# Long convolution and gated projection on one core: a GpSimd wait at the shared port, one pool of SBUF rooms, DRAM copies in another stage, GpSimd's tap in the last sequence

## The chip, the cores and the metric

The kernel runs on one core of a Trainium2 chip. The core has TensorE (in the profile PE for matrix products and PEld for weight loads), VectorE (DVE), ScalarE (ACT), GpSimd (POOL) and SyncE (SP, which here only issues DMAs). The metric is the device time of one execution in microseconds. All data are float32.

## The reference

For 8 sequences x of 6400 positions and 128 channels, the kernel computes a causal convolution with a filter h as long as the sequence (by Fourier transform), then a block with a short 5-tap convolution as gate and two 128 x 128 projections:

```python
L = 2 * S                                   # S = 6400
Xf = np.fft.rfft(x, n=L, axis=1)            # x: (8, 6400, 128)
Hf = np.fft.rfft(h, n=L, axis=0)            # h: (6400, 128)
x = np.fft.irfft(Xf * Hf[None], n=L, axis=1)[:, :S, :]
...
for k in range(5):
    gate_pre += conv_w[k][None, None, :] * xp[:, k:k + S, :]
gate = 1.0 / (1.0 + np.exp(-gate_pre))
val = x @ w_val
out = gate * val @ w_out
```

## The kernel before, in words

6400 is written as N1 x N2 = 100 x 64, and the transforms are products with constant matrices in four stages per sequence.

- **First stage** (`first_stage`, line 500): 16 groups of 8 channels. A group of x is loaded from DRAM into a room `x_sb` (4 rooms; at the start of the kernel 8 more in the place of the constant m4), TensorE makes 4 products of 200 columns, and ScalarE or VectorE copies the result into `gy`, in four pieces of 64x400.
- **Second stage** (`second`, line 546, and `product`, line 586): 13 blocks `kb` of 8 frequencies (the last has 4). A block needs a constant block `m2` (512 KB, `m2_load`, line 539) and the two blocks of the filter's spectrum (real and imaginary, 512 KB each, `h_load`, line 616), loaded from DRAM for every sequence. TensorE makes 8 products into two PSUM banks; ScalarE copies the result with halves swapped into a work room `w`; VectorE multiplies the PSUM result by the real part into `gy` (in the profile gy<-ps,h) and `w` by the imaginary part (w<-w,h); GpSimd adds the two (gy<-gy,w). In the last block VectorE adds.
- **Third stage** (loop over `q`, line 715): 32 groups of 4 products from `gy` into PSUM, copied to `dt` by ScalarE or VectorE. It starts when every add of the second stage is done. The first stage of the next sequence runs between its groups, since it writes `gy` where the third stage has read it.
- **Fourth stage** (loop over `CHUNKS`, line 827): 13 chunks of up to 5 cells of 100 positions. TensorE makes two products per cell with the constant `m4`; ScalarE copies the result to a room `y`; then come the taps: ScalarE starts sums in `dt` or `gl` (tap 4, and 3 as a product in `q`), VectorE adds three taps with scalar_tensor_tensor, and GpSimd adds `q` (dt<-dt,q or gl<-gl,q). In the last sequence VectorE adds four taps and GpSimd none. `gated` (line 786) follows for each chunk: sigmoid on ScalarE, projection by TensorE, gate on VectorE, second projection by TensorE, a copy out of PSUM and the store. The fourth stage and the next sequence's second stage run beside each other. Chunks with index `LAGGED` and above read `y` from SBUF and not the PSUM bank, and their taps and gate have due times in the next third stage.

**The head.** Before the first sequence the spectrum of h is computed by the same first two stages (`spectrum`, line 638) and stored to a DRAM tensor `hd`, and the first sequence's second stage runs beside it (`direct`, line 563). For blocks 0 to 4 both halves (64 partitions each) of the two planes are stored; for blocks 5 to 12 one half is, and a DRAM to DRAM copy doubles it (`hd<-hd`, lines 685 to 691, due times from `HEAD_END` on). Six groups of the next sequence's x (`STASH`) also go through the first stage here, into a part of m4's room.

**Rooms.** In SBUF there are 4 rooms for `m2` (`M2B`), 4 for h (`HB`) and 3 for `w` (`WB`), each 128 partitions x 4 KB. Each kind is used in turn: the n-th user waits for the (n - 4)th, or (n - 3)rd.

**What sets the order.** The program is a list of steps (`_Op`) with a cost, the steps that it follows, and a due time (`plan.base`). `_Plan.forward` (line 202) plays them through with modelled costs: each engine, when it is free, takes the ready step with the earliest due time that fits. The instructions are then issued to each engine in that order, and `_InOrder` (line 98) keeps it. On the chip each engine runs its own list in order; between engines there are only the waits that the data need. `port=True` marks steps whose VectorE or GpSimd instruction reads two operands in SBUF. The planner lets one of them run at a time and doesn't begin one on VectorE if the port is busy for over `PATIENCE` ns more (line 220). This is in the model alone: nothing on the chip ties GpSimd's instructions to VectorE's there.

```python
if o.port and e == "vector" and port > now + self.PATIENCE:
    return False
```

All instructions are issued through one helper, so every row of the profile has its line, L106; the rows are told apart by tile names and shapes.

Of the kernel before, what the change touches and what calls it, by code (L numbers as in the profile page):

```python
# [16 lines left out]
C = 128  # L17
# [17 lines left out]
LAGGED = 9  # L35
# [3 lines left out]
WB = 3  # L39
HB = 4  # L40
# [57 lines left out]
class _InOrder:  # L98
    def __init__(self, tc, engine):
        self._tc, self._engine = tc, engine  # L100

    def __getattr__(self, name):
        call = getattr(self._engine, name)

        def run(*args, **kwargs):
            return self._tc.keep_in_program_order(call(*args, **kwargs))  # L106

        return run


class _Engines:
    def __init__(self, tc):
        nc = tc.nc
        self.tensor, self.vector, self.scalar = (_InOrder(tc, e) for e in (nc.tensor, nc.vector, nc.scalar))
        self.gpsimd, self.sync = (_InOrder(tc, e) for e in (nc.gpsimd, nc.sync))
# [11 lines left out]

class _Op:
# [3 lines left out]
    def __init__(self, run, cost, after, bank=None, new=False, port=False):  # L132
        self.run, self.cost, self.bank, self.new, self.port = run, cost, bank, new, port
        self.after = [a for a in after if a is not None]
# [3 lines left out]
class _Plan:  # L138
# [4 lines left out]
    LEAD, LAND, AHEAD = 1500, 2000, 1200  # L143
# [58 lines left out]
    def forward(self):  # L202
# [3 lines left out]
        halves = [[0] * 2 for _ in range(4)]  # L206
        self.split = False
        port = server = now = 0
        events, began = [], []
        for o in self.ops:  # L210
            o.at = None
            if o.bank is not None:
                o.bank.left, o.bank.seen, o.bank.spot = len(o.bank.users), [], None

# [20 lines left out]
        while left:  # L235
            moved = True
            while moved:
                moved = False
                for e in free:
# [26 lines left out]
                    if o.port and e in ("vector", "gpsimd"):  # L266
                        port = now + dur
                    b = o.bank
                    if b is not None:
                        if o.new:  # L270
                            i, h = b.spot = self.room(b, halves, now)
                            self.split = self.split or b.n == 1
# [42 lines left out]
    def room(self, b, halves, now):  # L315
# [5 lines left out]
        if not self.split and not all(all(p) for p in free[2:]):  # L321
            return None
        spot = next(((i, h) for i in (2, 3) for h in (0, 1) if free[i][h]), None)
# [24 lines left out]
def _dma(kb):  # L348
    return 330, kb * 1024 / 400
# [7 lines left out]
def longconv_moe(ctx: ExitStack, tc: tile.TileContext, x, h, r1, m2, r3, m4, w64, out):  # L357
# [19 lines left out]
    y_t = [cp.tile([128, CH, N1], F32, name=f"y_{i}") for i in range(YB)]  # L377
    y_head = cp.tile([128, HEAD[1], N1], F32, name="y_head")
    m2_sb = [cp.tile([128, KB, C], F32, name=f"m2_{i}") for i in range(M2B)]
# [615 lines left out]
```

## Time and profile before

| what | us |
|---|---|
| median of 3 timed runs | 1075.39 (1075.15 to 1077.14) |
| the profiled execution, its own time | 1071.16 |
| span of its instructions | 1069.4 |
| outside the span | 1.76 |
| TensorE busy | 1046.7 |
| VectorE busy | 764.7 |
| ScalarE busy | 773.4 |
| GpSimd busy | 390.6 |

A row of a view by stretches has the stretch, its length, the busy time and the number of instructions (x) of each engine, the granted share of TensorE's clock (PEclk), the share of time that the 16 DMA engines are busy, and GB/s. A row of a group of instructions has engine, operation, what it writes and reads, shapes and count; then its busy time and the mean of one in ns; then the idle time of its engine ahead of it and what ended that. A row of the timeline has its start, its length, and in brackets the idle time before it and what ended it. A float32 product appears as two MATMUL and two LDWEIGHTS records.

The span falls into a head up to about 106 us; seven rounds of about 126 us (third stage of a sequence with the first stage of the next, then its fourth stage with the next one's second stage), of which the third stages begin at about 106, 216, 342, 467, 594, 720 and 846 us; and the last sequence, whose third stage begins at 971 us and which has no next one.

### The profile page before, as it was taken

Reading aid. Unit: us, or ns where it says so; the run is one execution under the profiler, and the core shown is the slowest. Engines: PE = TensorE matmul, PEld = TensorE weight load, DVE = VectorE, ACT = ScalarE, POOL = GpSimd, SP = SyncE. Lnnn points to the kernel's source line nnn. Section 1 sums busy time; section 2 is a strip of 40 time slices with the busy share of each in tenths; the row PEclk is TensorE's granted clock in tenths of the full one; section 3 lists DMA queues with packets and bytes.
Section 4 is the critical chain, followed back from the end, with each engine's and each line's share of the span. In section 5 each row is a group of like instructions: output and inputs, shape, how many; then the busy total and the mean of one; then the engine's idle time right before and its main releaser. Section 6 shows DMA issues by size and latency. Waiting matters only on the chain.

```text
span 1069.4 us, 19629 instructions
## 1 busy us (share of the span) xinstructions
PE 1046.7 (98%) x7488; PEld 941.8 (88%) x7488; DVE 764.7 (72%) x1059; ACT 773.4 (72%) x1282; POOL 390.6 (37%) x225
## 2 busy tenths in 40 slices
PE   9998999999999999999999999999999999999997
PEld 9998998889988899888988799888998889988983
DVE  6999259963698647985498835987379763997197
ACT  5687678866887669866787568876688666887553
POOL 0077107820286105750077201861048410674000
PEclk9999999999999999999999999999999999999999
DMA  9499939933498227962299424993269731891012
GB/s 270 135 361 364 280 85 355 365 135 87 148 383 318 92 83 258 381 215 97 78 348 373 132 88 124 375 335 107 80 217 385 246 95 47 298 331 49 27 49 76
DMA packets 80459, 221.14 MB, mean 207 GB/s; under 512 B 9514, under 2 KB 24846, under 8 KB 80142
## 3 DMA queue, kind: packets, MB, share of 16 engines
q1 hardware_dynamic: 80366, 219.89, 59.3%
q8 instruction: 59, 0.97, 0.4%
q14 instruction: 34, 0.28, 0.1%
HBM read 184.47 MB, written 39.32 MB: 209 GB/s over the span
## 4 chain that ended last, share of the span: by engine, by line
PE 74%; DVE 10%; DMA 8%; issue 3%; ACT 2%; POOL 1%; SPq 0%; DVEq 0%; POOLq 0%
PE pb L106 46%; PE ps L106 28%; DMA h<-hd 6%; DVE dt L106 3%; DVE gy L106 3%; DVE gl L106 2%; DVE w L106 1%; POOL gy L106 1%; ACT w L106 1%; DMA hd<-hd 1%; DMA m_sb<-hl 1%; DMA gl<-w 1%; ACT dt L106 1%; POOL gl L106 0%; DMA x<-xl 0%
## 5 line engine op out<-in xcount | busy, mean ns | idle before, releaser
L106 ACT COPY gy<-ps 64x400 f32<-64x400 f32 x436 | 211.9, 486 | 111.1 <-PE ps L106 107.3
L106 PEld LDWEIGHTS pb<-r_sb,gy 128*100 128x100 f32 x2048 | 239.4, 171 | 31.6 <-issue 24.4
L106 POOL TENSOR_TENSOR gy<-gy,w 128x1024 f32<-128x1024 f32 x96 | 230.9, 2406 | 76.9 <-DVE w L106 61.9
L106 PEld LDWEIGHTS pb<-m_sb,dt 100*128 100x128 f32 x1968 | 232.4, 193 | 19.6 <-issue 17.8
L106 PE MATMUL pb<-r_sb,gy 128*100 128x128 f32 x2048 | 245.7, 273 | 2.6 <-ACT gl L106 2.2
L106 PE MATMUL pb<-m_sb,dt 100*128 100x100 f32 x1968 | 234.3, 275 | 0.7 <-ACT dt L106 0.7
L106 DVE COPY dt<-pb 100x512 f32<-100x512 f32 x162 | 112.0, 691 | 149.5 <-PE pb L106 133.6
L106 PEld LDWEIGHTS ps<-gy,m 128*128 128x128 f32 x1600 | 194.9, 188 | 23.0 <-issue 16.3
L106 PE MATMUL ps<-gy,m 128*128 128x128 f32 x1600 | 201.5, 278 | 1.7 <-DVE gy L106 1.0
L106 PE MATMUL ps<-r_sb,x 100*128 100x200 f32 x992 | 186.9, 333 | 3.4 <-DMA x<-xl 2.2
L106 PEld LDWEIGHTS ps<-r_sb,x 100*128 100x128 f32 x992 | 165.8, 190 | 13.1 <-issue 11.0
L106 DVE SCALAR_TENSOR_TENSOR dt<-pb,w_sb,dt 128x500 f32<-128x500 f32 (+7 forms) x216 | 131.6, 626 | 9.0 <-issue 4.9
L106 DVE TENSOR_TENSOR w<-w,h 128x1024 f32<-128x1024 f32 (+1 forms) x91 | 119.3, 1311 | 12.5 <-DMA h<-hd 12.3
L106 DVE TENSOR_TENSOR gy<-ps,h 128x1024 f32<-128x1024 f32 (+1 forms) x100 | 117.3, 1176 | 10.2 <-DMA h<-hd 9.6
L106 ACT COPY y<-pb 128x500 f32<-128x500 f32 x136 | 77.1, 571 | 60.1 <-PE pb L106 51.9
L106 POOL TENSOR_TENSOR dt<-dt,q 128x500 f32<-128x500 f32 (+3 forms) x56 | 90.2, 1611 | 60.3 <-ACT w L106 41.9
L106 ACT ACTIVATE w<-ps 64x1024 f32<-64x1024 f32 (+1 forms) x91 | 89.9, 988 | 30.2 <-issue 18.7
L106 POOL MEMSET dt<- 128x4 f32 x8 | 0.8, 104 | 303.4 <-PE pb L106 303.4
L106 POOL TENSOR_TENSOR gl<-gl,q 128x500 f32<-128x500 f32 (+1 forms) x42 | 52.7, 1254 | 113.4 <-DVE gl L106 101.2
L106 PE MATMUL pb<-y,w_sb 128*128 128x500 f32 x178 | 91.1, 594 | 0.7 <-ACT y L106 0.7
L106 ACT COPY w<-ps 64x1024 f32<-64x1024 f32 (+1 forms) x91 | 88.4, 971 | 1.5
L106 DVE SCALAR_TENSOR_TENSOR gl<-y,w_sb,gl 128x500 f32<-128x500 f32 (+1 forms) x108 | 77.3, 727 | 13.3 <-POOL gl L106 10.8
(65 smaller groups left out, 915.2 us busy)
## 6 DMA issues: line engine op xcount, KB each, us to landing
h<-hd SPq DMA_DIRECT2D x168, 512.0 KB, 6.2
m<-m SPq DMA_DIRECT2D x96, 512.0 KB, 6.0
x<-xl SPq DMA_DIRECT2D x116, 224.0 KB, 2.6
out<-y SPq DMA_DIRECT2D x89, 250.0 KB, 4.5
hd<-h SPq DMA_DIRECT2D x8, 512.0 KB, 5.9
hd<-hd SPq DMA_DIRECT2D x14, 256.0 KB, 6.3
h<-hd SPq DMA_DIRECT2D x14, 256.0 KB, 4.5
m_sb<-xl SPq DMA_DIRECT2D x12, 224.0 KB, 6.6
```

The source lines that it names most:

```text
L106: return self._tc.keep_in_program_order(call(*args, **kwargs))
```

## The change

1. **GpSimd waits for VectorE at the port.** `_Engines` keeps a list of the instructions made. When the program is issued, a GpSimd step marked `port` gets a dependency, by semaphore, on the last instruction of the last VectorE step marked `port` that stands before it in the plan and has not been used for this yet.
2. **One pool of rooms.** The 4 + 4 + 3 rooms become 11 rooms `k_t` (`SLOTS`); a step that needs one takes any free room when the planner places it (`_Slot`, `take`), and it is free again when the last user is done. Loads leave one room free (`spare=1`); m2 still has at most 4 blocks at a time. The head has two rooms more, as before. The first rooms for x grow by four (in `y`), and the loads for the stash use them.
3. **The last adds.** `summed` may be placed on VectorE or GpSimd for block 11 of a second stage that has h loaded (`MANY = 2`); block 12 stays on VectorE.
4. **DRAM copies.** The copies that double blocks 5 to 12 are due in the first third stage, and each pair waits for a group of that stage, from the fifth on.
5. **The last sequence.** Chunks 1 to 9 (`LASTQ = 10`) have GpSimd's tap there too, ahead of VectorE's taps (`LAST3`). The last chunk is cut in two, of 3 and 2 cells. It has 11 + 6 rooms for y, as 7 + 6 before.
6. **The planner's numbers.** New due times, `LAGGED` 8 for 9, `LAST_LAG` 10 for 9, `PATIENCE` 380 for 143, one warming product less, `LAND` 2200 for 2000, a DMA at 375 for 400 bytes per ns. One-bank steps may take a free two-bank room before the small ones exist, and the first third stage may use the two-bank rooms.

```diff
-LAGGED = 9
+LAGGED = 8
...
-WB = 3
-HB = 4
+SLOTS = 11
+MANY = 2
...
-THIRD = 50165
-FOURTH = 5190
-SECOND = 4398
-GATE = 9690
-LAGS = 10092
-EARLY = -3528
-PATIENCE = 143
-ROUSE = 4
-LAST = 3839
-LAST_GATE = 8804
-LAST_LAG = 9
+THIRD = 44275
+FOURTH = 4511
+SECOND = 3959
+GATE = 13466
+LAGS = 9341
+EARLY = 545
+PATIENCE = 380
+ROUSE = 3
+LASTQ = 10
+FIRST3 = 0
+LAST3 = 1
+LAST = 3177
+LAST_GATE = 12434
+LAST_LAG = 10
...
+class _Slot:
+    def __init__(self, head=False):
+        self.users, self.head, self.place = [], head, None
...
+        def open_slots(o):
+            n = len(slots) if o.take.head else SLOTS
+            return [i for i in range(n) if slots[i] is not None and slots[i] <= now]
...
+            if any(s.spot is None for s in o.wait) or o.take is not None and len(open_slots(o)) <= o.spare:
+                return False
...
+                    if o.take is not None:
+                        i = o.take.spot = min(open_slots(o), key=lambda i: (i < SLOTS, slots[i]))
+                        slots[i] = None
+                    for s in [*o.use, *([o.take] if o.take else [])]:
+                        s.left -= 1
+                        if not s.left:
+                            slots[s.spot] = max(u.done for u in s.users)
...
-    m2_sb = [cp.tile([128, KB, C], F32, name=f"m2_{i}") for i in range(M2B)]
-    h_sb = [cp.tile([128, KB * C], F32, name=f"h_{i}") for i in range(HB)]
+    k_t = [cp.tile([128, KB * C], F32, name=f"k_{i}") for i in range(SLOTS)]
     x_sb = [cp.tile([PX, XG, N2], F32, name=f"x_{i}") for i in range(XB)]
-    w_t = [cp.tile([128, KB * C], F32, name=f"w_{i}") for i in range(WB)]
...
+    spare += [t[:PX] for t in y_sb[:4]]
...
+    def summed(kb, w, u, after, many):
+        where = {"gpsimd": _pool(count(kb) * C)}
+        if kb == NKB - 1:
+            where = {}
+        if kb >= NKB - many:
+            where["vector"] = _dve(count(kb) * C)
+        return add(
+            lambda e: getattr(nc, e).tensor_tensor(out=u, in0=u, in1=kdt(w.ap(), kb), op=ADD),
+            where, after, port=True, use=[w],
+        )
...
-    for g in range(NG):
-        kb = WHOLE + g
-        plan.where, plan.base = f"double {kb}", HEAD_END + 2500 * g
-        if kb < NKB:
-            n = count(kb) * C
-            lo, hi = slice(0, N2), slice(N2, 2 * N2)
-            stored[kb][0] = [dma(hd[kb, 0, hi, :n], hd[kb, 0, lo, :n], n // 4, stored[kb][0])]
-            stored[kb][1] = [dma(hd[kb, 1, lo, :n], hd[kb, 1, hi, :n], n // 4, stored[kb][1])]
+    def double(kb, after):
+        n = count(kb) * C
+        lo, hi = slice(0, N2), slice(N2, 2 * N2)
+        for r, (o, i) in enumerate(((hi, lo), (lo, hi))):
+            stored[kb][r] = [dma(hd[kb, r, o, :n], hd[kb, r, i, :n], n // 4, [*stored[kb][r], *after])]
...
+        for kb in range(WHOLE, NKB if b == 0 and nxt else 0):
+            plan.where, plan.base = f"double {kb}", begin + 2500 * (kb - WHOLE)
+            double(kb, [s3[4 + 2 * (kb - WHOLE)]])
...
+        chunks = CHUNKS if nxt else [*CHUNKS[:-1], (CHUNKS[-1][0], 3), (CHUNKS[-1][0] + 3, CH - 3)]
...
-            if nxt:
+            by_pool = nxt or i < LASTQ
+            if by_pool:
...
+            if not by_pool or not (FIRST3 if nxt else LAST3):
+                taps()
...
+                if FIRST3 if nxt else LAST3:
+                    taps()
...
+    held = None
     for op in plan_ops:
...
+        nc.made.clear()
         op.run(op.engine)
+        if op.port and op.engine == "vector":
+            held = nc.made[-1]
+        elif op.port and op.engine == "gpsimd" and held is not None:
+            tc.add_manual_dep(nc.made[0], held.name, sync, reason="the port is VectorE's")
+            held = None
```

More of the change, by code (lines that the diff above doesn't have):

```diff
@@ L125, in ap, with __init__ @@
         return self.place
+class _Slot:
+    def __init__(self, head=False):
+        self.users, self.head, self.place = [], head, None
+    def ap(self):
+        return self.place
 class _Op:
-    def __init__(self, run, cost, after, bank=None, new=False, port=False):
+    def __init__(self, run, cost, after, bank=None, new=False, port=False, take=None, use=(), wait=(), spare=0):
         self.run, self.cost, self.bank, self.new, self.port = run, cost, bank, new, port
+        self.take, self.use, self.wait, self.spare = take, list(use), [*use, *wait], spare
+        for s in [*self.use, *([take] if take else [])]:
+            s.users.append(self)
         self.after = [a for a in after if a is not None]
@@ L320, in room @@
             return next(((i, 0) for i, p in enumerate(free) if all(p) and (i < 2 or not self.split)), None)
-        if not self.split and not all(all(p) for p in free[2:]):
-            return None
-        spot = next(((i, h) for i in (2, 3) for h in (0, 1) if free[i][h]), None)
+        spot = None
+        if self.split or all(all(p) for p in free[2:]):
+            spot = next(((i, h) for i in (2, 3) for h in (0, 1) if free[i][h]), None)
         if spot is None and b.wide:
@@ L406, in spectral, with dma, run @@
         return bank.ap().rearrange("p b (k d t) -> p d (b k) t", t=2, d=C // 2)
-    def dma(o, i, kb, after=(), early=0):
-        return add(lambda e: nc.sync.dma_start(o, i), {"sync": _dma(kb)}, after, early=early)
+    def dma(o, i, kb, after=(), early=0, **more):
+        def run(e):
+            nc.sync.dma_start(*(a() if callable(a) else a for a in (o, i)))
+        return add(run, {"sync": _dma(kb)}, after, early=early, **more)
     def cells(y, n):
@@ new lines, in swap, with times_im @@
+            nc.scalar.activation(t[:N2], v[N2:], AF.Copy, scale=1.0 if kb < WHOLE else -1.0)
+            nc.scalar.copy(t[N2:], v[:N2])
+        def times_im(e):
+            t = kdt(w.ap(), kb)
+            nc.vector.tensor_tensor(out=t, in0=t, in1=kdt(hs[1].ap(), kb), op=MUL)
+        c = _times(_act(n, held=True), 2)
+        s = add(swap, {"scalar": (c[0] + 95, c[1])}, [p], bank=bank, take=w, wait=hs)
+        a = times_re(kb, p, bank, hs, u, h_ready[:1])
+        b = add(times_im, {"vector": _dve(n)}, [s, h_ready[1]], port=True, use=[hs[1], w])
@@ L625, in gy_at @@
+        return summed(kb, w, u, [a, b], MANY)
+    def h_load(kb):
+        k, hs = count(kb) * C, [_Slot(), _Slot()]
+        ops = []
+        for r, slot in enumerate(hs):
+            ops.append(dma(
+                lambda slot=slot: slot.ap()[:, :k], hd[kb, r, :, :k], k // 2, [*head_done, *stored[kb][r]], 6000,
+                take=slot, spare=1,
+            ))
+        return hs, ops
     def gy_at(g):
@@ L660, in spectrum @@
+        stored.append([[x] for x in st])
         return p, hs, [r0, r1_], [i0, i1], st
@@ L909, in part @@
                 return o, lambda: view(k, k + o.shape[1])
[L911 to L913 removed]
+            k4 = max(0, min(n, HEAD[0] - a - 4))
+            if k4:
+                first(4, [part(o, k) for k, o in cells(a + 4, k4)], gl_free(a + 4, k4), a + 4, k4)
+            by_pool = nxt or i < LASTQ
+            if by_pool:
                 qi = len(q_user)
```

212 lines of the change are left out of this document (96 added, 116 removed).

## The prediction

> **What bounds the kernel now.** I read the page first, then the busy time by stretches, then the timeline where TensorE (PE) is idle, then the groups of instructions.
>
> ```profile
> span 1069.4 us, 19629 instructions
> PE 1046.7 (98%) x7488; PEld 941.8 (88%) x7488; DVE 764.7 (72%) x1059; ACT 773.4 (72%) x1282; POOL 390.6 (37%) x225
> ```
>
> PE is busy 98% of the span, and the change neither adds nor removes a matrix product worth naming. So a gain can come only out of PE's idle time, 1069.4 - 1046.7 = 22.7 us, and out of stretches in which its clock is low. The next view cuts the span where the third stage of a sequence begins (six windows of 12 us, then 960), and at head and tail.
>
> ```profile
> core 0: us, PE busy (x) PEld busy (x) DVE busy (x) ACT busy (x) POOL busy (x), PEclk, DMA share, GB/s
> 0.00:94.00 94.00, 92.45 (x652) 90.86 (x653) 82.33 (x118) 67.71 (x100) 33.78 (x25) 1.00 0.82 270
> 94.00:106.00 12.00, 8.14 (x49) 7.15 (x48) 11.52 (x14) 8.66 (x17) 7.88 (x5) 1.00 1.00 378
> ...
> 206.00:218.00 12.00, 10.83 (x78) 9.00 (x78) 11.18 (x13) 7.43 (x12) 5.96 (x3) 1.00 0.98 342
> ...
> 332.00:344.00 12.00, 10.90 (x82) 9.20 (x81) 11.97 (x14) 8.10 (x14) 9.87 (x6) 1.00 0.93 333
> ...
> 457.00:469.00 12.00, 11.04 (x83) 9.34 (x83) 11.97 (x15) 8.09 (x14) 9.48 (x5) 1.00 0.93 324
> ...
> 582.00:594.00 12.00, 10.64 (x66) 8.68 (x64) 11.49 (x12) 5.64 (x10) 7.71 (x4) 0.86 0.86 286
> ...
> 710.00:722.00 12.00, 10.17 (x73) 8.34 (x72) 11.58 (x14) 6.95 (x13) 5.99 (x3) 1.00 0.81 264
> ...
> 834.00:846.00 12.00, 10.44 (x68) 8.85 (x67) 9.89 (x12) 5.75 (x10) 8.52 (x6) 0.86 0.84 300
> ...
> 960.00:972.00 12.00, 11.84 (x90) 10.15 (x89) 11.43 (x13) 8.70 (x15) 10.65 (x6) 1.00 0.26 86
> ...
> 1050.00:1066.00 16.00, 13.14 (x32) 5.02 (x31) 12.06 (x19) 6.18 (x13) 0.00 (x0) 0.89 0.21 77
> ```
>
> Window less PE's busy time: 1.55 us before 94; 3.86 us at 94 to 106; 1.17, 1.10, 0.96, 1.36, 1.83, 1.56 and 0.16 us at the seven boundaries, 8.14 in all; 2.86 us at 1050 to 1066. The clock is below 1 in three of these windows:
>
> ```profile
> 588.56:592.20 3.64, 3.64 (x13) 2.72 (x13) 3.60 (x5) 0.00 (x0) 2.41 (x2) 0.54 0.80 240
> 841.40:845.00 3.60, 3.60 (x12) 2.60 (x13) 3.35 (x5) 0.00 (x0) 2.37 (x2) 0.53 0.73 253
> 1059.70:1063.50 3.80, 3.80 (x6) 1.62 (x6) 1.49 (x3) 1.52 (x3) 0.00 (x0) 0.55 0.12 46
> ```
>
> 3.64 x 0.46, 3.60 x 0.47 and 3.80 x 0.45 are 1.7 us each, 5.1 in all: work that counts as busy and takes twice its time. So what can be won is 3.9 (head) + 8.1 + 3.4 (boundaries) + 2.9 + 1.7 (tail) = 20.0 us.
>
> **Why PE is idle at a boundary.** The third stage needs every product of the second stage, and the last of them are late:
>
> ```profile
> 581.57 1.51 DVE L106 TENSOR_TENSOR w<-w,h 128x1024 f32<-128x1024 f32 x1 [1.90 <-DMA h<-hd]
> 584.13 3.05 DVE L106 TENSOR_TENSOR w<-w,h 128x1024 f32<-128x1024 f32 x1
> 583.73 2.37 POOL L106 TENSOR_TENSOR gy<-gy,w 128x1024 f32<-128x1024 f32 x1
> 588.56 1.73 PE L106 MATMUL pb<-dt,w_sb 128*128 128x500 f32 x2 [1.36 <-ACT gl L106]
> L106 DVE TENSOR_TENSOR gy<-ps,h 128x1024 f32<-128x1024 f32 x92 | 111.9, 1219 | 10.2 <-DMA h<-hd 9.6 <-ACT q L106 0.3
> L106 DVE TENSOR_TENSOR w<-w,h 128x1024 f32<-128x1024 f32 x84 | 109.5, 1303 | 11.7 <-DMA h<-hd 11.5
> L106 POOL TENSOR_TENSOR gy<-gy,w 128x1024 f32<-128x1024 f32 x96 | 230.9, 2406 | 76.9 <-DVE w L106 61.9 <-PE ps L106 7.3 <-PE pb L106 7.1
> L106 POOL TENSOR_TENSOR dt<-dt,q 128x500 f32<-128x500 f32 x35 | 72.0, 2057 | 18.1 <-DVE dt L106 11.0 <-PE pb L106 2.8 <-ACT dt L106 2.2
> L106 DVE TENSOR_TENSOR w<-w,h x91: 804/1218/3049, 160.0 to 968.8; 128x1024 f32<-128x1024 f32 x84, 128x512 f32<-128x512 f32 x7
> L106 POOL TENSOR_TENSOR gl<-gl,q 128x500 f32<-128x500 f32 x35 | 45.0, 1285 | 113.4 <-DVE gl L106 101.2 <-ACT y L106 12.2
> ```
>
> VectorE (DVE) first waits 1.90 us for a block of h, then its next w product, 1.22 us long where nothing holds it (the same size from PSUM: 1219 ns), takes 3.05 us, because GpSimd's (POOL) add began 0.4 us earlier and holds the port to its end. 1.90 + 1.83 = 3.7 us of lateness leave PE idle for 1.36, and at 588.56, where that gap ends, the first low stretch begins. The other direction is dearer: GpSimd's tap takes 2057 ns where it meets such a product and 1285 where it mostly doesn't, 0.77 x 35 = 27 us of GpSimd's time in seven sequences.
>
> **The change, part by part.** *One pool of rooms.* The second stage is close to what DMA gives:
>
> ```profile
> 533.00:588.00 55.00, 53.80 (x404) 47.63 (x402) 49.57 (x59) 46.50 (x67) 40.66 (x21) 1.00 0.96 358
> 533.00:589.00 56.00, 41.66 (x21) 1.00 0.96 355
> h<-hd SPq DMA_DIRECT2D x168, 512.0 KB, 6.2
> ```
>
> (The second row is GpSimd alone.) Before, loads own 4 rooms for m2 and 4 for h, 8 in all, and 3 rooms lie empty between stages. After, loads may take all but one of 11: 10 rooms, 2 more, of 524 kB each. 1.05 MB at 355 GB/s are 3.0 us of DMA moved out of each second stage into the third, where DMA is not full. The 1.90 us wait above would be gone. *The last adds.* Block 11 may be added by DVE: about 1.3 us instead of 2.41, so the third stage can begin up to 1.1 us earlier. *The wait.* GpSimd waits for DVE's last port product before it in the plan. For an add that product is mostly its own input, so nothing changes; a tap waits by semaphore where it now waits at the port. It costs nothing where the port would have held it (cover: the 0.77 us), and the length of the product, up to 1.3 us, where GpSimd would have been first; what stands behind it are the next adds and taps on POOL, then sigmoid, gate and PE's projection. It takes reversals away, of which DVE shows (1303 - 1219) x 84 = 7.1 us. Chunk 8 is lagged now: three more products (0.73 us each) per sequence hold the port, and the plan lets DVE begin up to 0.38 us before the port is free (0.14 before). The other new constants set order alone.
>
> Boundaries together: between nothing and 8.1 + 3.4 = 11.5 us. Each gap (0.2 to 1.8 us) is shorter than the 3.0 us of DMA or 1.1 + 1.8 us of port that the change takes off its chain, but a new order brings gaps of its own (the bad end is the backfire, below). I take half of the idle time and both half-clock stretches: 4.1 + 3.4 = **-7.5 us**.
>
> *DRAM copies.* At the end of the head:
>
> ```profile
> 103.12 0.49 SPq L106 DMA_DIRECT2D hd<-hd  x1
> 103.77 0.46 SPq L106 DMA_DIRECT2D m<-m  x1
> 104.27 0.47 SPq L106 DMA_DIRECT2D hd<-hd  x1
> 105.71 1.08 PE L106 MATMUL ps<-r_sb,x 100*128 100x200 f32 x5 [2.23 <-DMA x<-xl]
> hd<-hd SPq DMA_DIRECT2D x14, 256.0 KB, 6.3
> 106.00:148.00 42.00, 42.00 (x335) 41.80 (x334) 13.36 (x20) 26.28 (x51) 5.11 (x6) 1.00 0.70 213
> ```
>
> The copies stand between the loads of x on SP's queue, at a DMA share of 1.00, and PE waits 2.23 us for x. After, they come from the fifth group of the third stage on, and x has four more rooms. I take the 2.2 us and leave the other 1.6 of the 3.86 (waits for evictions): **-2.2 us**, between 0 and -3.9. The third stage has room: 16 copies, each at most 0.26 MB read and 0.26 written, are 8 MB, 23 us at 355 GB/s at the very most and 11 if read and write overlap; 30% of 42 us is 12.6, and some copies lie in it already. On SP they are 16 issues of 0.49 us, 7.8 us of the stage, ahead of loads of x, m4 and h. If they don't fit, x or m4 is late there, for up to the 2.2 us that it cost before: the term is then 0.
>
> *Tail.* DVE is the late engine there, and the start is quoted beside it:
>
> ```profile
> 1059.69 1.03 PE L106 MATMUL pb<-gl,w_sb 128*128 128x500 f32 x1 [1.46 <-DVE gl L106]
> L106 DVE SCALAR_TENSOR_TENSOR gl<-y,w_sb,gl 128x500 f32<-128x500 f32 x100 | 73.5, 735 | 12.1 <-POOL gl L106 10.8
> L106 ACT ACTIVATE q<-pb,w_sb 128x500 f32<-128x500 f32 x56 | 38.2, 683 | 0.0
> 1.18 3.78 PE L106 MATMUL ps<-q 128*128 128x256 f32 x8 [1.18 <-DVE q L106]
> ```
>
> Nine chunks of the last sequence give one tap each (735 ns on DVE, 6.6 us in all) to GpSimd, which has nothing to do at 1050 to 1066; ScalarE gets nine activations of 683 ns, 6.1 us, spread over a stretch in whose last 16 us it is busy for 6.18. Taking 6.6 us off DVE ahead of the 1.46 us gap removes most of 2.9 + 1.7; the last chunks (one of them now in two pieces of 3 and 2 cells, some more small instructions) still go by DVE alone. **-3.0 us**, between +1.3 (GpSimd's tap, 1285 ns, now stands ahead of DVE's three, where no other chunk covers it) and -4.6. *The start*: one of four warming products less, of 3.78 us together, and x has then to be there 0.9 us sooner. I take 0, between -0.9 and +0.9 (the first real products at half the clock for as long).
>
> Sum: 7.5 + 2.2 + 3.0 = 12.7 us. The profiled execution took 1071.16 us (span 1069.4 and 1.76 around it), the median of the timed runs is 1075.39, 4.23 more, which I keep: 1071.16 - 12.7 + 4.23 = **1062.7**.
>
> **Rivals.** *The gaps move.* In one second stage of 56 us the port is booked for GpSimd's 41.7 less 27/7 = 3.9 held, and DVE's 13 products, 12 x 1.219 + 0.80 = 15.4: 53 us. The new due times ask for 13 x 3.959 = 51.5. If the port sets the stage, PE's gaps stay 8.1 + 3.4 and only head and tail gain: 1075.39 - 5.2 = **1070.2**. For it: 53 of 56. Against: an add moved to DVE takes 1.1 us off that sum, and the DMA wait ahead of the gap isn't the port's.
>
> *The clock falls anyway.* Two of the seven boundaries have the low clock, and the longest gap, 1.83 us in the window from 710, has none (PEclk 1.00). If the stretches don't hang on these gaps they stay, and the sum is 12.7 - 3.4 = 9.3: **1066.1**. For it: that window. Against: the two low stretches begin at boundaries, the third right after a gap. [...]
>
> *The wait backfires (slower).* GpSimd runs in order, so when DVE's product waits for h, a tap behind it now waits too, and everything behind the tap. DVE's w products waited 11.5 us for h; if all of it passes to the third stage's start, and the five boundaries that had no half-clock stretch get one (5 x 1.7 = 8.5), the sum is +11.5 + 8.5 - 5.2 = +14.8: **1090.2**. It decides from where the wait in a sequence is longer than GpSimd's free time, (56 - 53)/13 = 0.23 us per block. For it: that is little. Against: the pool brings h earlier, and an add waits for its product anyhow.
>
> *The wait does nothing.* GpSimd is held at the port already (2057 against 1285 ns); if the plan's order holds without it and the pool's loads fill the same time, the gaps stay, and new gaps of the new order (three half-clock stretches, 5.1) eat head and tail: **1075.4**. [...]
>
> **How the numbers follow.** Forecast 0.49 (1055 to 1068); the clock falls anyway 0.08; gaps move 0.20; nothing 0.09; backfires 0.14. Low end: all terms at their best, 20.0 + 0.9, 1054.5. High end: the edge of no change, 1077.5; beyond both lies about 0.2 (the backfire and a little). A measurement of this kernel can tell 0.2%, 2.15 us: faster 0.49 + 0.08 + 0.20 = 0.77, same 0.09, slower 0.14.
>
> **What would show it.** Right: PE's idle time near 12 us less; no clock of 0.53 after a boundary; no wait of PE on x near 105; the w products near 1.22 us; GpSimd busy after 972, DVE's gaps of PE gone there. Wrong: boundaries that lose over 1 us again (gaps moved), longer waits of GpSimd on DVE with PE's gaps over 2 us (backfire), or PE waiting for x or m4 at 106 to 150.

## The result, and the profile after

| | before | after |
|---|---|---|
| median of the timed runs, us | 1075.27 (4 runs, 1070.99 to 1077.14) | 1047.89 (4 runs, 1047.48 to 1050.34) |
| profiled execution, us | 1071.16 | 1047.48 |
| its span, us | 1069.4 | 1045.7 |
| span less PE's busy time, us | 22.7 | 8.5 |

The ratio is 0.9756, with an interval of 0.9723 to 0.9788: the change takes 27.4 us away. The forecast was 1062.7 with a range of 1054.5 to 1077.5, so a gain was foreseen; it came out twice as large, and the time 6.6 us below the low end.

The first lines of the page, and its line on the chain that ended last (shares of the span by engine; before, PE had 74%, DVE 10% and DMA 8%). In the changed kernel the helper that issues all instructions stands on line 109.

```profile
span 1045.7 us, 19783 instructions
PE 1037.2 (99%) x7490; PEld 937.5 (90%) x7490; DVE 752.1 (72%) x1033; ACT 794.1 (76%) x1322; POOL 347.7 (33%) x229
...
PE 92%; DVE 6%; issue 1%; ACT 1%; POOL 0%; DVEq 0%; POOLq 0%; ACTq 0%
```

DMA is gone from the chain. The stretches at the starts of the third stages (now at 104, 212, 336, 459, 582, 705, 829 and 952 us), with the columns of the same view as before:

```profile
0.00:94.00 94.00, 92.55 (x654) 90.51 (x654) 82.73 (x119) 68.48 (x101) 34.19 (x25) 1.00 0.85 269
94.00:106.00 12.00, 10.07 (x62) 9.55 (x63) 11.68 (x14) 9.40 (x20) 7.53 (x5) 1.00 0.85 268
204.00:216.00 12.00, 12.00 (x91) 10.47 (x90) 10.19 (x13) 8.53 (x15) 4.98 (x4) 1.00 0.99 352
328.00:340.00 12.00, 12.00 (x89) 10.49 (x88) 10.13 (x13) 7.44 (x14) 4.86 (x4) 1.00 1.00 371
...
697.00:709.00 12.00, 12.00 (x90) 10.47 (x89) 10.79 (x14) 7.95 (x14) 4.24 (x4) 1.00 1.00 367
...
944.00:956.00 12.00, 12.00 (x93) 10.46 (x92) 10.21 (x13) 8.33 (x15) 4.97 (x4) 1.00 0.13 45
956.00:1028.00 72.00, 72.00 (x511) 60.55 (x511) 42.42 (x72) 49.38 (x90) 16.59 (x16) 1.00 0.11 39
1028.00:1043.00 15.00, 13.41 (x49) 7.16 (x48) 11.61 (x23) 7.57 (x17) 0.00 (x0) 1.00 0.32 121
```

PE has no idle time in the windows at the seven later boundaries, and its clock stays 1.00. Of the 8.5 us that PE is still idle, all but 0.85 lie before 148 us and after 957.

Where the time came from, by the starts of the third stages in both profiled executions:

| part of the span | before, us | after, us | difference |
|---|---|---|---|
| head, to the first third stage | 108.5 | 104.3 | -4.2 |
| first round | 110.2 | 108.2 | -2.0 |
| six more rounds | 752.7 | 739.3 | -13.3 |
| last sequence | 98.0 | 93.9 | -4.2 |
| span | 1069.4 | 1045.7 | -23.7 |

By the timeline the first two third stages of the kernel before begin at 108.5 and 218.7 us, and not at about 106 and 216 as said above. Eight products of the next sequence's first stage, 1.35 us, now stand behind the start of the first third stage and not ahead of it; so of the head's 4.2 us only 2.9 were won, and the first round won 1.35 more than its row says.

The other 3.7 us are not in the span: the median of the timed runs lay 4.1 us above the profiled execution before (1075.27 against 1071.16) and lies 0.4 above it now. The six later rounds took 123.9 to 127.0 us before; now each of them takes 123.2.

The groups of GpSimd and of VectorE's two products, and VectorE's adds by tile, which answer to the rows of before:

```profile
L109 POOL TENSOR_TENSOR gy<-gy,k 128x1024 f32<-128x1024 f32 x89 | 211.4, 2379 | 69.7 <-PE pb L109 38.1 <-DVE k L109 28.2 <-DMA k<-hd 1.3
L109 DVE TENSOR_TENSOR k<-k,k 128x1024 f32<-128x1024 f32 x84 | 120.2, 1431 | 0.0
L109 DVE TENSOR_TENSOR gy<-ps,k 128x1024 f32<-128x1024 f32 x89 | 108.4, 1219 | 11.4 <-ACT k L109 9.3 <-PE ps L109 1.0 <-DMA out<-y 0.2
L109 POOL TENSOR_TENSOR dt<-dt,q 128x500 f32<-128x500 f32 x40 | 50.0, 1249 | 41.1 <-DVE k L109 28.0 <-ACT k L109 7.5 <-PE pb L109 3.6
L109 POOL TENSOR_TENSOR gl<-gl,q 128x500 f32<-128x500 f32 x37 | 46.1, 1247 | 141.1 <-DVE gl L109 132.6 <-ACT q L109 5.5 <-ACT dt L109 3.0
...
L109 DVE TENSOR_TENSOR gy<-gy,k x14: 676/946/1215, 210.0 to 950.5; 128x1024 f32<-128x1024 f32 x7, 128x512 f32<-128x512 f32 x7
```

Three readings. GpSimd's tap takes 1249 ns, not 2057, and waits 28.0 us for DVE instead: what it lost inside its record at the port it now waits ahead of it. No product of DVE waits for a block of h (9.6 + 11.5 us before). And seven adds of 128x1024 are DVE's, one in each second stage, block 11's. But the second product (k<-k,k, before w<-w,h) is not shorter: 1431 ns against 1303, so DVE is now held for (1431 - 1219) x 84 = 17.8 us in all, against 7.1. The gain can't come from DVE being held for less time; e1 below shows that it matters which instruction is held.

### The profile page after: what moved, and what is told of

Its sections match the earlier page's. It is cut to its first block, busy times and chain, and to the rows that moved or that the text cites. A ratio compares the mean times of both kernels' runs of the same rounds, so it can differ in the third digit from the quotient of the medians.

```text
span 1045.7 us, 19783 instructions
## 1 busy us (share of the span) xinstructions
PE 1037.2 (99%) x7490; PEld 937.5 (90%) x7490; DVE 752.1 (72%) x1033; ACT 794.1 (76%) x1322; POOL 347.7 (33%) x229
## 4 chain that ended last, share of the span: by engine, by line
PE 92%; DVE 6%; issue 1%; ACT 1%; POOL 0%; DVEq 0%; POOLq 0%; ACTq 0%
PE pb L109 58%; PE ps L109 34%; DVE k L109 2%; DVE gy L109 2%; DVE dt L109 1%; DVE gl L109 0%; POOL gy L109 0%; ACT k L109 0%; ACT m_sb L109 0%; ACT dt L109 0%; ACT y_head L109 0%; ACT y L109 0%; DVE q L109 0%; DVEq L109 0%; POOLq L109 0%
## 5 line engine op out<-in xcount | busy, mean ns | idle before, releaser
L109 POOL TENSOR_TENSOR gy<-gy,k 128x1024 f32<-128x1024 f32 x89 | 211.4, 2379 | 69.7 <-PE pb L109 38.1
L109 PEld LDWEIGHTS ps<-gy,k 128*128 128x128 f32 x1600 | 195.1, 188 | 23.0 <-issue 17.6
L109 PE MATMUL ps<-gy,k 128*128 128x128 f32 x1600 | 201.3, 278 | 0.4 <-ACT k L109 0.4
L109 ACT ACTIVATE k<-ps 64x1024 f32<-64x1024 f32 (+1 forms) x101 | 99.7, 987 | 36.7 <-PE ps L109 33.7
L109 DVE TENSOR_TENSOR k<-k,k 128x1024 f32<-128x1024 f32 (+1 forms) x91 | 124.5, 1374 | 0.0
L109 DVE TENSOR_TENSOR gy<-ps,k 128x1024 f32<-128x1024 f32 (+1 forms) x96 | 113.2, 1180 | 11.9 <-ACT k L109 9.3
L109 ACT COPY k<-ps 64x1024 f32<-64x1024 f32 (+2 forms) x109 | 104.7, 961 | 5.2 <-PE ps L109 2.6
L109 DVE SCALAR_TENSOR_TENSOR gl<-y,w_sb,gl 128x500 f32<-128x500 f32 (+3 forms) x122 | 85.6, 708 | 31.2 <-POOL gl L109 29.4
L109 POOL TENSOR_TENSOR dt<-dt,q 128x500 f32<-128x500 f32 (+1 forms) x64 | 66.2, 1036 | 107.9 <-ACT k L109 43.5
L109 ACT COPY y<-pb 128x500 f32<-128x500 f32 (+1 forms) x126 | 71.2, 565 | 32.0 <-PE pb L109 25.3
```

Of the source, the lines that this page charges most:

```text
L109: r = self._tc.keep_in_program_order(call(*args, **kwargs))
```

## The experiments

Medians are compared with the changed kernel's 1047.89. They are safer than the ratios here: the kernel before spread from 1065.5 to 1081 us over its runs, and its median from 1068.73 to 1075.27 over the five groups of runs, while each kernel with the changed structure stayed within 4. Differences of 1 or 2 us between kernels whose runs overlap are not shown to be differences.

| kernel | median, us | ratio to before (interval) | against the changed kernel |
|---|---|---|---|
| no wait (e1) | 1055.05 | 0.9857 (0.9817 to 0.9896) | +7.2 |
| rooms by kind (e3) | 1053.11 | 0.9830 (0.9789 to 0.9872) | +5.2 |
| block 11's add on GpSimd (e4) | 1054.50 | 0.9847 (0.9809 to 0.9885) | +6.6 |
| no GpSimd tap in the last sequence (e6) | 1052.64 | 0.9813 (0.9789 to 0.9837) | +4.7 |
| copies in the head (e5) | 1048.09 | 0.9776 (0.9753 to 0.9799) | +0.2 |
| no extra rooms for x (e12) | 1048.64 | 0.9773 (0.9691 to 0.9855) | +0.8 |
| patience 143 (e9) | 1049.74 | 0.9785 (0.9716 to 0.9853) | +1.9 |
| the old numbers (e7) | 1082.92 | 1.0094 (1.0073 to 1.0115) | +35.0 |
| before + the wait (e2) | 1067.81 | 0.9945 (0.9912 to 0.9978) | +19.9 |
| before + the new numbers (e8) | 1066.30 | 0.9940 (0.9919 to 0.9961) | +18.4 |
| before + numbers + wait (e10) | 1065.40 | 0.9926 (0.9895 to 0.9958) | +17.5 |
| ... + block 11's add on DVE (e13) | 1064.99 | 0.9948 (0.9919 to 0.9977) | +17.1 |
| ... + GpSimd's tap in the last sequence (e14) | 1060.06 | 0.9891 (0.9823 to 0.9960) | +12.2 |

All of them compute the whole output.

**The wait, taken away.** In the theory (theory A) it stops GpSimd from taking the port ahead of a product that something waits for. The rival (theory B below) says that GpSimd was held there already (2057 ns against 1285), so that the wait does nothing.

```diff
-            tc.add_manual_dep(nc.made[0], held.name, sync, reason="the port is VectorE's")
```

> The changed kernel with the same planned order and without the wait of GpSimd on VectorE. Theory A (the wait pins the planned order at the port, and that is what closed the gaps of TensorE at the boundaries): VectorE is held by GpSimd's instructions in places the plan did not mean, the gaps come back, some 5 to 15 us slower than with the wait (1053 to 1063 us). Theory B (the pool of rooms brings h in time, the port lock does the waiting anyway): the wait does nothing, within 2 us of 1047.9. GpSimd's taps dt<-dt,q go back to some 2.06 us in both.

The time was 1055.05, 7.2 us more: the rival falls. GpSimd's tap and DVE's product are both longer without the wait (1249 and 1431 ns with it):

```profile
L109 POOL TENSOR_TENSOR dt<-dt,q 128x500 f32<-128x500 f32 x40 | 76.5, 1912 | 16.1 <-DVE dt L109 10.4 <-PE pb L109 3.6 <-PE ps L109 1.0
L109 DVE TENSOR_TENSOR k<-k,k 128x1024 f32<-128x1024 f32 x84 | 124.3, 1479 | 0.0
```

Both kernels issue the same instructions in the same order, so the same place can be read in both. The timeline without the wait:

```profile
536.25 1.99 DVE L109 TENSOR_TENSOR k<-k,k 128x1024 f32<-128x1024 f32 x1
537.11 2.24 POOL L109 TENSOR_TENSOR dt<-dt,q 128x500 f32<-128x500 f32 x1
...
538.39 1.22 DVE L109 TENSOR_TENSOR gy<-ps,k 128x1024 f32<-128x1024 f32 x1
539.31 2.37 POOL L109 TENSOR_TENSOR gy<-gy,k 128x1024 f32<-128x1024 f32 x1
539.53 3.23 DVE L109 TENSOR_TENSOR k<-k,k 128x1024 f32<-128x1024 f32 x1
...
544.21 1.51 PE L109 MATMUL pb<-dt,w_sb 128*128 128x400 f32 x2 [1.12 <-DVE dt L109]
```

and that of the changed kernel, where the same instructions come 1.36 us earlier:

```profile
534.89 1.99 DVE L109 TENSOR_TENSOR k<-k,k 128x1024 f32<-128x1024 f32 x1
...
537.02 1.23 DVE L109 TENSOR_TENSOR gy<-ps,k 128x1024 f32<-128x1024 f32 x1
537.04 1.26 POOL L109 TENSOR_TENSOR dt<-dt,q 128x500 f32<-128x500 f32 x1 [1.25 <-ACT k L109]
538.16 1.23 DVE L109 TENSOR_TENSOR k<-k,k 128x1024 f32<-128x1024 f32 x1
...
539.62 4.71 POOL L109 TENSOR_TENSOR gy<-gy,k 128x1024 f32<-128x1024 f32 x2 [1.31 <-PE pb L109]
...
541.56 1.06 PE L109 MATMUL pb<-dt,w_sb 128*128 128x400 f32 x4
```

Without the wait the tap starts at 537.11, meets the product that runs to 538.24, and shows 2.24 us for 1.26 us of work. It ends at 539.35, the add behind it on GpSimd follows at once, and it takes the port 0.2 us ahead of the next product. That one takes 3.23 us instead of 1.23, the gate's products behind it on DVE come 2.0 us late, and PE idles 1.12 us. With the wait the tap runs clear of the first product, the add waits for the second, and both are out of the way. (The add's row names PE for its idle time, but the add starts 0.23 us behind the end of DVE's product, 538.16 + 1.23.) The same product of 3.23 us and the same gap of 1.1 us behind it stand once in each of five rounds, near 296, 544, 670, 796 and 921 us: 5.6 us of the 7.2. After two of them, in the profiled execution (1057.41 us, the longest of the four), the clock is halved (a stretch without the wait; the other, from 670.40, has 0.54):

```profile
544.20:547.80 3.60, 3.59 (x13) 2.94 (x14) 3.41 (x4) 0.66 (x2) 2.40 (x2) 0.53 0.86 323
```

In these rows the instruction that starts second is the long one: the tap of 2.24 us ends 1.11 us behind the product's end (1.26 us is its length with the wait), and the product of 3.23 us ends 1.08 us behind the add's end at 541.68 (1.23 us with the wait). So the rival is right that GpSimd was held, but what it made of that does not follow: here the one that came first held up the other, and the wait decides who comes first. The theory was wrong about the place, though. The gaps do not stand at the boundaries, where it put them, but at a gate's projection in the middle of the second stage: the one at 544 us lies 42 us ahead of the next third stage.

**The wait alone, on the kernel before.**

```diff
...
+        if op.port and op.engine == "vector":
+            held = nc.made[-1]
+        elif op.port and op.engine == "gpsimd" and held is not None:
+            tc.add_manual_dep(nc.made[0], held.name, sync, reason="the port is VectorE's")
+            held = None
```

> The kernel before with nothing added but the wait of GpSimd on VectorE, its order unchanged. Theory A: the products w<-w,h stop being held (mean 1303 to about 1220 ns) and part of the 13 us lost at the boundaries is won, 4 to 10 us faster than before. Theory B: within 0.2% of before, since the late blocks of h are still late. The rival that the wait backfires: slower, as a late product now holds the taps too.

1067.81, 5.8 us less than the kernel before in the same group of runs (1073.62), with the tap at 1250 ns: the wait helps by itself, on an order made without it. The sign that was named is half there: the w products fell from 1303 to 1271 ns and not to 1220, and DVE still waits 17.3 us for h.

**Rooms by kind, in the changed kernel** (4 for m2, 4 for h, 3 for w, none left free).

```diff
-            n = len(slots) if o.take.head else SLOTS
-            return [i for i in range(n) if slots[i] is not None and slots[i] <= now]
+            n = {"m": range(4), "h": range(4, 8), "w": range(8, 11)}[o.take.kind]
...
+            return [i for i in n if slots[i] is not None and slots[i] <= now]
```

> The changed kernel with its 11 rooms split again by kind: 4 for m2, 4 for h, 3 for w (the head's two more rooms go to h, as before), all else as changed, the order planned anew. Theory B: VectorE's waits for h come back (21.9 us before, none after), and with them gaps at the boundaries, 5 to 13 us slower than the changed kernel. Theory A: most of the gain stays, under 4 us slower.

1053.11, 5.2 us more, at the low edge of theory B's range. DVE waits for h again, 7.4 us in 8 waits, and PE idles ahead of the second third stage (a group of DVE, then the timeline of PE):

```profile
L109 DVE TENSOR_TENSOR gy<-ps,k 128x1024 f32<-128x1024 f32 x89 | 108.1, 1215 | 14.0 <-DMA k<-hd 7.4 <-ACT k L109 6.3
...
212.69 1.53 PE L109 MATMUL pb<-r_sb,gy 128*100 128x128 f32 x12 [1.47 <-DVE gy L109]
```

The six later rounds take 0.3 to 0.6 us longer each. The profiled execution was the shortest of the four, 1050.30 us, so these gaps account for 2.8 us. The other three took 1052.18 to 1054.19 at a granted clock of 0.998, where the profiled one had 1.000; 0.002 x 1053 is 2.1 us, so half-clock stretches may be most of the rest, which no profile shows.

**Block 11's add left to GpSimd.**

```diff
-MANY = 2
+MANY = 1
```

> The changed kernel with block 11's add on GpSimd again. The last add ends some 1.1 us later in each of seven sequences. If that add is on the path to the third stage, up to 7 x 1.1 = 7.7 us slower; if TensorE has other work there (theories A and B alike leave it open), under 2 us.

1054.50, 6.6 us more, with about 0.9 us lost at each of the seven starts of a third stage (timeline of PE):

```profile
710.40 1.86 PE L109 MATMUL pb<-r_sb,gy 128*100 128x128 f32 x15 [1.03 <-DVE gy L109]
```

Seven times 0.9 is 6.3, nearly the whole difference.

**No GpSimd tap in the last sequence.**

```diff
-LASTQ = 10
+LASTQ = 0
```

> The changed kernel without GpSimd's tap in the last sequence; VectorE adds four taps there, the last chunk stays cut in two. By the prediction's step: the tail loses 3 us or more again (the tail lost 7.5 us against full pace before and 2.0 after), 3 to 5.5 us slower than the changed kernel. If the new due times and the cut chunk did it: under 1 us.

1052.64, 4.7 us more. PE's timeline at the end shows why:

```profile
1038.80 1.10 PE L109 MATMUL pb<-gl,w_sb 128*128 128x500 f32 x2 [1.61 <-DVE gl L109]
...
1041.94 1.11 PE L109 MATMUL pb<-gl,w_sb 128*128 128x500 f32 x2 [1.20 <-DVE gl L109]
...
1046.87 0.94 PE L109 MATMUL pb<-gl,w_sb 128*128 128x400 f32 x2 [0.74 <-DVE gl L109]
```

DVE's sums are late by 3.6 us in all; in the changed kernel PE waits 0.23 and 0.49 us in the tail.

**The copies back in the head.**

```diff
-        for kb in range(WHOLE, NKB if b == 0 and nxt else 0):
-            plan.where, plan.base = f"double {kb}", begin + 2500 * (kb - WHOLE)
-            double(kb, [s3[4 + 2 * (kb - WHOLE)]])
...
+    for g in range(NG):
+        kb = WHOLE + g
+        plan.where, plan.base = f"double {kb}", HEAD_END + 2500 * g
...
```

> The changed kernel with the DRAM copies due at the end of the head again, all else as changed, the order planned anew. By the prediction's step: TensorE waits some 2.2 us for x near 105 us, 1.5 to 3 us slower than the changed kernel, and the boundaries stay without gaps. If the first third stage was hurt by the copies instead: faster.

1048.09, 0.2 us more, within the spread: the wait of 2.2 us that was expected did not come back. PE's product there has no wait for x, though the copies are where they were:

```profile
103.55 1.52 PE L109 MATMUL ps<-r_sb,y 100*128 100x200 f32 x8
```

**The four extra rooms for x, taken away**, as the next suspect.

```diff
-    spare += [t[:PX] for t in y_sb[:4]]
...
-            i = (n % 4, 12 + n % 4)[n // 4 % 2]
+            i = n % 4
```

> The changed kernel without the four more rooms for x (the stash's loads use the four rooms of before), copies in the third stage as changed. With the copies back in the head TensorE didn't wait for x. If the rooms for x were what ended that wait: it comes back here near 105 us, 1.5 to 3 us slower than the changed kernel. If either of the two is enough: within 1 us.

1048.64, within the spread too, and no wait of PE near 105 either (one of 0.98 us came at 136). So neither is needed alone. Both undone together in the changed kernel wasn't tried, but e8 below has neither and bears on it.

**The numbers.** The changed kernel with all due times and model constants of before, except the warming products, which this kernel keeps at three:

```diff
...
-THIRD = 44275
-FOURTH = 4511
-SECOND = 3959
-GATE = 13466
...
+THIRD = 50165
+FOURTH = 5190
+SECOND = 4398
+GATE = 9690
...
```

> The changed kernel's structure with the due times, LAGGED, LAST_LAG, PATIENCE and DMA costs of before. Theory C (the numbers alone made the order better): back to 1068 to 1075 us. Theories A and B (wait and rooms): most of the gain stays, 1050 to 1062 us.

1082.92: outside both ranges, and a miss for all three theories. With the old numbers the new structure is 0.94% slower than the kernel before, and PE's idle time in the span is 1080.9 - 1050.0 = 30.9 us. So the new structure as a whole wins nothing with the old numbers, though the wait by itself did (e2). The other way round, the kernel before with the new numbers:

```diff
...
-THIRD = 50165
-FOURTH = 5190
...
+THIRD = 44275
+FOURTH = 4511
...
```

> The structure of before (rooms by kind, no wait on the chip, copies in the head, no tap of GpSimd in the last sequence) with the due times, LAGGED, LAST_LAG, PATIENCE and DMA costs of after. Theory C: 1048 to 1060 us. Theories A and B: within 8 us of before, either side, 1066 to 1082 us, with the gaps at the boundaries still there.

1066.30, 6.8 us less than before in that group of runs (1073.07), within the range of theories A and B: the numbers without the new structure win no more than that. Most rounds lose only about 1 us then, but one third stage waits for a late sum (PE's timeline):

```profile
219.40 2.85 PE L106 MATMUL pb<-r_sb,gy 128*100 128x128 f32 x12 [4.89 <-DVE gy L106]
```

This kernel also settles most of the question of x. Its copies are in the head and x has no extra rooms, as in the kernel before; only the numbers are new. PE's wait for x, 2.23 us before, is 0.30 (PE's timeline), and 0.39 in e10 below:

```profile
104.57 1.59 PE L106 MATMUL ps<-r_sb,x 100*128 100x200 f32 x8 [0.30 <-DMA x<-xl]
```

So the new order alone takes nearly all of that wait away, without the copies' move and without the rooms.

One number by itself, the planner's patience at the port:

```diff
-PATIENCE = 380
+PATIENCE = 143
```

> The changed kernel with PATIENCE 143 for 380, the order planned anew: the plan no longer lets VectorE begin up to 0.38 us before the port is free. If the slack at the port is part of the gain: VectorE idles at the port, gaps at the boundaries, 3 to 10 us slower. If the other numbers carry it: under 2 us.

1049.74, 1.9 us more with runs from 1048.12 to 1050.98, which overlap those of the changed kernel (1047.48 to 1050.34): no difference is shown.

**Building up from before.** The old structure with the new numbers and the wait (the edits of e2 and e8 together):

```diff
...
-SECOND = 4398
+SECOND = 3959
...
+            tc.add_manual_dep(nc.made[0], held.name, sync, reason="the port is VectorE's")
```

> The structure of before with the new numbers and with the wait on the chip. The wait alone was worth some 5.8 us and the numbers alone some 6.8. If the two add up: 1058 to 1063 us, and the rest to the changed kernel is rooms, last adds and tail. If the wait is worth more with an order made for it: under 1058. If both remove the same gaps: 1064 to 1067.

1065.40. The wait was worth 5.8 on the old numbers; here it is worth 0.9, which the spread of both kernels covers. So their gains don't add, as the third of the alternatives had it. Next, block 11's add on DVE as well:

```diff
             where = {"vector": _dve(n)}
+        if kb == NKB - 2:
+            where["vector"] = _dve(n)
```

> The structure of before with the new numbers, the wait on the chip, and block 11's add of a second stage with h loaded allowed on VectorE. Six boundaries of the same kernel without the last lose 0.87 us each where the third stage waits for the last adds. If the parts add up: those go, 5 to 6 us faster than 1065.4, 1059 to 1061. If the rooms by kind bring new late blocks of h instead: within 2 us of 1065.4.

1064.99, 0.4 us less, within the spread: 5 to 6 us were expected if the parts add up. PE's waits at the later boundaries did shrink, from 0.71 us each to about 0.2, but the gap before the second third stage grew, from 4.55 us (e10) to 5.86. Then GpSimd's tap in the last sequence too:

```diff
-            if nxt:
+            by_pool = nxt or i < 10
+            if by_pool:
...
```

> The one before with GpSimd's tap in the last sequence too, ahead of VectorE's (no cut of the last chunk). If the parts add up: 4 to 5 us less again, 1054 to 1057, and what is left to the changed kernel (1047.9) is the pool of rooms and the gap of 4.7 us ahead of the second third stage. If the tail's gain needs the pool's y rooms: under 2 us.

1060.06, 4.9 us less, the size that e6 gave the tap, and without the cut of the last chunk. The range named, 1054 to 1057, was missed, since it was counted from e13's. What still parts this kernel from the changed one, 12.2 us, is the pool, the copies with the rooms for x, the small parts (PSUM banks, a warming product, the cut chunk), and what hangs on them. The largest gap left is the same one (timelines of GpSimd, DVE and PE):

```profile
217.08 1.74 POOL L106 TENSOR_TENSOR gl<-gl,q 128x500 f32<-128x500 f32 x1 [2.95 <-DVE gy L106]
...
218.85 0.74 DVE L106 SCALAR_TENSOR_TENSOR gl<-y,w_sb,gl 128x500 f32<-128x500 f32 x1 [1.13 <-POOL gl L106]
...
220.34 2.00 PE L106 MATMUL pb<-r_sb,gy 128*100 128x128 f32 x8 [5.31 <-DVE gy L106]
```

Ahead of this gap stands a chain through GpSimd. Its tap at 217.08 comes right behind an add of DVE that it doesn't read (gy, the semaphore's wait), DVE idles 1.13 us for the tap, and the last add of the second stage stands behind that. Whether the tap could have come earlier without the wait no run tells; DVE's add ran from 215.79 to 217.00 us. DVE's products wait 7.6 us for h in that kernel, but only 0.55 of it in the 11 us ahead of this gap. That the pool alone would close the gap was not tried.

**Gaps made on purpose.** In before and in e1 idle times of 1.0 to 1.6 us were followed by half the clock in some places (0.50 behind 1.36 us in before, 0.53 behind 1.12 us in e1) and not in others (1.00 behind 1.49 us in before). So 18 pauses were put into third stages of the changed kernel, by 2 to 18 small copies on GpSimd that PE has to wait for:

```diff
...
+            for _ in range(gap):
+                nc.gpsimd.tensor_copy(scratch[:, 32:], scratch[:, :32])
+            idle = list(nc.made)
+            tc.add_manual_dep(idle[0], last_pe.name, sync, reason="TensorE's last")
...
+            tc.add_manual_dep(nc.made[0], idle[-1].name, sync, reason="the gap")
```

> The changed kernel with 18 idle gaps put into TensorE's stream in the third stages (three in each of six sequences, 2 to 18 small GpSimd copies long, which only TensorE's next product waits for). It tells how long a gap makes the clock fall. If gaps of 1.2 us and over do: the granted clock falls to about 0.5 for some 3.6 us after the longer ones, 1.7 us more each. [...]

One execution was taken, of 1134.78 us. Windows with a gap and what follows it, in two places:

```profile
247.40:249.00 1.60, 0.38 (x4) 0.36 (x4) 0.00 (x0) 1.50 (x4) 0.85 (x4) 1.00 0.24 50
249.00:254.00 5.00, 5.00 (x39) 4.52 (x38) 2.25 (x4) 2.38 (x5) 0.00 (x0) 1.00 0.25 73
264.40:266.50 2.10, 0.35 (x3) 0.35 (x4) 0.00 (x0) 1.95 (x4) 1.26 (x6) 1.00 0.31 108
266.50:270.00 3.50, 3.50 (x19) 3.50 (x18) 1.14 (x2) 0.00 (x0) 0.00 (x0) 0.51 0.00 1
```

After 1.60 - 0.38 = 1.22 us the clock stays 1.00; after 2.10 - 0.35 = 1.75 it is 0.51 for the next 3.5 us. Of the 18, those of 0.67, 1.22, 1.22 and 1.40 us had no fall, and all 14 from 1.76 us up had one (the 16 records behind a gap take 2.00 us after those four, 2.88 to 3.74 after the 14), of 3.41 us after ten of them and of 6.83 after the four of 2.86, 2.91 and twice 5.04 us. The sum fits: 55.1 us of gaps and half of 10 x 3.41 + 4 x 6.83 us are 85.8, and the kernel took 86.9 longer than the changed one.

## Why the prediction was wrong, point by point

**Right.** The kernel was bound by PE's gaps and half-clock stretches; the boundaries' term was the largest; with h loaded earlier and block 11's add on DVE the gaps there went (e3, e4); idle time fell by 14.2 us where "near 12" was named; no half clock is left at a boundary; GpSimd works after the last third stage begins (16.59 us at 956 to 1028).

**Where the 14.8 us between forecast and time lie.** The rounds gave 15.3 us for 7.5, the head 4.2 for 2.2, the last sequence 4.2 for 3.0, and of the 4.23 us kept between profiled execution and median 0.4 are there: 7.8 + 2.0 + 1.2 + 3.8.

**The step that failed: "I take half of the idle time".** The half-clock stretches went as forecast, 3.4 us. But from the first third stage's start to the last one's PE was idle for 10.3 us (8.0 of them in the windows up to 846 us) and is idle for 0.85 now: 9.4 us came where 4.1 was taken. The prediction's own rows said that each gap is shorter than what the change takes off its chain; the half was a discount for gaps that a new order might bring, for which no row stood, and the new order brought next to none.

**The premise above it failed too: "a gain can come only out of PE's idle time" and the low clock, 20.0 us at most.** Idle time fell by 14.2 us and half-clock time by 5.1, 19.3 together, but the span fell by 23.7. One warming product is 0.85 of the rest. The other 3 to 4 us were gaps that PE's records cover: the last record before a gap ends later than its successor would have begun in an unbroken run. The gap ahead of 588.56 is 1.36 us by the records; from the start of the product before it to the start of the one behind it there are 1.52 us more than in an unbroken run. Counted so over all products, half-clock stretches included, PE lost 32 to 35 us before, 19 to 20 of them between 148 and 957 us, and loses 9 to 11 now (4 to 5 there); how large each is depends on which distance is taken as unbroken. The work itself is the same within 1 us.

**"For an add that product is mostly its own input, so nothing changes"** failed. The add in the pair of timelines waits for the product of the *next* block, not its own, and that is where the wait earns its 7.2 us: not at a boundary, but at five places in the middle of second stages. The term counted only the tap.

**"It takes reversals away"**, with "the w products near 1.22 us" as its sign, failed as a measure: they rose to 1431 ns. With the same order and no wait they take 1479 (e1), so the wait does take holding away, 4 us of it; the new order brings more than that, in places where PE does not come to wait.

**Head copies, -2.2.** The wait for x went, but not because the copies moved: with them back in the head the time is the same (e5), and with the new numbers alone 0.30 of the 2.23 us is left (e8). Of the 4.2 us by which the first third stage starts earlier, 2.0 are less waiting and 0.85 the warming product, which the forecast put at 0 ("The start"); 1.35 are only the eight products that now stand behind the start.

**The tail, -3.0.** The mechanism was right and the size short: the tap is worth 4.7 us (e6) or 4.9 (e14), and the last sequence takes 4.2 us less. The 4.2 lie within the bound of -4.6, the tap's own gain just beyond it: the term was set too low within its range.

**The 4.23 us between profiled execution and median were kept** without a reason, and 0.4 of them is there. This alone is 3.8 of the 6.6 us by which the time lies below the low end. The kernel before varied by 15 us from run to run, the changed one by 3. The executions of the kernel before that stand beside the experiments show what varies: the three with a granted clock of 1.000 took 1066.29 to 1069.12 us, the four with 0.985 to 0.987 took 1076.89 to 1080.96, and (1 - 0.987) x 1070 is 14 us. So most of that spread is half-clock time, and the changed kernel has 1.000 in all four of its executions. For the kernel before, the executions behind the 4.1 us have no clock on record except the profiled one (0.995), so that their 4.1 us are of this kind is likely, but not shown.

**The rivals.** "The gaps move" because GpSimd and DVE book 53 of 56 us at the port: GpSimd now takes 32.43 us of the second stage at 532 to 588, where it took 41.66, and PE doesn't idle there:

```profile
532.00:588.00 56.00, 56.00 (x413) 48.97 (x412) 52.31 (x64) 44.28 (x66) 32.43 (x18) 1.00 0.98 363
```

Of the 9.2 us of difference 4.7 are two adds fewer in the stretch (block 11's, now DVE's, and one that falls outside it), and 4.0 are what five taps had waited at the port and shown as work (0.81 us each). "The clock falls anyway" did not happen. "The wait backfires" did not happen in the changed kernel: GpSimd does wait 28.0 us for DVE ahead of its taps, but PE has only 0.85 us of idle time in the rounds. In e14 there is a place as the rival describes it, a tap behind DVE's add and DVE idle 1.13 us for the tap, but no run shows that the wait is what made the tap late. "The wait does nothing" is refuted by e1.

**Why the parts don't add.** Undone one at a time, wait, rooms, add and tap cost 7.2 + 5.2 + 6.6 + 4.7 = 23.7 us. That this is also what the span lost is chance, since the numbers undone alone cost 35.0. Added to the old structure, numbers and wait win 8.7 together (1074.15 - 1065.40), and the add 0.4 more, which is nothing. Rooms and add act at one place, the start of a third stage, which waits for the last of several things: in e13 the later boundaries gained by the add, and the gap before the second third stage took it back. The wait acts elsewhere (e1). How much of the last 12.2 us each remaining part holds stays open, and so does why the numbers fit one structure and not the other.

## What to carry to other kernels

Where PE is the bound, measure its loss from start to start of its products too, and not only by what its records leave idle: here idle time and half-clock stretches account for 19.3 of the 23.7 us that the span lost. Where instructions of two engines hold each other up, as here a product of 1.23 us that took 3.23 beside GpSimd's add, look not at how long each is held but at which instruction is held, and who waits for it; a semaphore on the less urgent engine can fix that order (7.2 us here). Parts that end in the same wait must be tried by undoing each from the whole, since alone they may show nothing, and due times tuned for one structure can turn another one slower (1082.92). Where executions of a kernel differ, look at their granted clocks before you keep the difference in a forecast.

## What the runs showed of the hardware

A GpSimd record includes its time at the port: the same 128x500 sum shows 2057 ns where it meets DVE's products, and 1249 ns where it is kept clear of them (1912 with the same order of instructions and no wait, e1). A half-clock stretch of the rounds lasts 3.41 us in the kernel before, at a granted clock of 0.50 (from 588.85 and from 841.44 us); behind the made gaps of e11 it lasts 3.41 or 6.83 us. The length of a gap alone does not tell whether one follows: in the kernel before, the gaps of 1.36 and 1.56 us that end at 588.56 and 841.36 had one, and that of 1.49 us that ends at 715.96 had none; in e1 two of the five gaps of 1.1 us had one; of the made gaps the four of 0.67 to 1.40 us had none and the 14 of 1.76 us and more had one each time. What decides between 1.1 and 1.76 us no run shows.
